# Three of a pair's weight sums added by DMA for one batch, and raw weights fetched from another queue

## The chip, the cores and the metric

The kernel runs on one core of one Trainium2 chip. The metric is the device time of one execution in microseconds (us). Times of several executions are given as a median; the profile is of one execution.

The engines are named as in the profile: PE is TensorE's matmul, PEld its loading of weights, DVE is VectorE, ACT is ScalarE, POOL is GpSimd, SP is SyncE, which here issues DMAs only. Each engine works through its own queue in order.

## The reference

Attention with a hash mask, then a Fourier mixing block with a two-layer network. Cut to what matters:

```python
# B, H, S, D = 4, 8, 768, 64; proj is 64 x 6; w_ch1 is 512 x 2048, w_ch2 is 2048 x 512
mask   = bucket(q @ proj)[:, :, :, None] == bucket(k @ proj)[:, :, None, :]   # 6 sign bits each
scores = where(mask, q @ k.T / 8, -1e9)
attn   = softmax(scores) @ v
x      = attn laid out as (B, S, 512)
mixed  = real(fft(fft(x, axis=1), axis=2))
u      = x + mixed
un     = (u - mean(u)) / sqrt(var(u) + 1e-6)
out    = u + relu(un @ w_ch1) @ w_ch2
```

The two network weights arrive as 64-bit floats and are narrowed on the chip; the other inputs are 32-bit floats.

## The kernel before

**Attention.** For each batch `b` (0 to 3), `attention(b)` goes through four pairs of heads (`n = 4 * b + t`), and in each pair through six chunks `c` of 128 keys. One chunk is one step of the generator. `weigh(n, c)` makes the scores of both heads for all 768 queries on TensorE (line 869), takes their exponential on ScalarE into a `pk` tile (line 873), and, for pairs that are not in `LITE = (0, 1, 2, 3, 4)`, multiplies by the hash mask on VectorE (line 879). In the `LITE` pairs the mask is put into the scores by a matmul with bits. There are two `pk` tiles (`NPK = 2`), used in turn, 128 partitions by 2 x 2 x 385 values, of which 384 of each 385 are weights.

The weights of a chunk go two ways. `values` multiplies them with v on TensorE (line 890). And their sum over all keys is needed for the softmax: VectorE adds the chunks into the tile `acc` (line 964; 128 x 1536 values, one buffer), for chunk 1 as the sum of the first two chunks' tiles, for later chunks as `acc` plus the new tile. In batch 0 the addition is made in two halves, and the last chunk is left to TensorE. When the six chunks are done, TensorE adds `acc` over the keys with `ones` (line 908), and `scale` divides by the sum and writes the tile `x` (lines 915 to 929).

**Mixing.** `mix(b)` runs beside `attention(b + 1)`: a fixed number of its steps is taken after each step of the attention. It folds `x`, makes the two Fourier transforms by matmuls (lines 1062 and 1091), normalises, and runs the network in `mlp7`, in which both products are made by the seven-product scheme of Strassen and Winograd: `inner` for the first layer (line 1366) and `outer7` for the second (line 1246). `spread` makes the reciprocal deviations `rs`, partly on GpSimd (lines 1127 and 1128). The seven operands that come from the first layer's weights are made on VectorE in `quarters` (lines 1164 to 1167), for batch 0 just ahead of their use, and are stored to the DRAM tile `ad` by SP; later batches fetch them back through a ring (`w<-ad`, line 1339). The second layer's operands go the same way through `bd` (lines 1217 and 1251).

**Raw weights.** The class `Arrival` fetches raw 64-bit weights, 512 KB at a time, into a few raw buffers (`zraw`, `fraw`) and narrows each with `narrow` (ScalarE lines 639, 646 and 647, VectorE lines 631 to 644). `convert(i)` narrows slice `i` and then issues the fetch of slice `i + depth` into the buffer that it has read, so that this DMA waits for the last instruction on that buffer. `weights1` does so for the first layer beside `attention(0)`, with seven raw buffers; its first seven fetches are issued by SP. `weights2` does so for the second layer beside batch 1's attention, with two raw buffers. All further fetches are issued by GpSimd (line 685). Besides these, GpSimd's queue carries in this part of the run the `rs` instructions, one small memset of `F` and the stores of batch 0's output (line 1000).

**Loads.** `load(n + 1)` is called at the start of pair `n` and issues q, k and v of the next pair from SP (lines 556, 562 and 570): in all 14 DMAs, most of them of 48 or 96 KB in short runs.

**Order.** In the part that holds `prepare(0)`, `attention(0)` and `weights1`, the order on PE, DVE, ACT and POOL is the order of the program, by a `manual_schedule`; SP is not in that list. From batch 1's attention on, a planner that simulates the engines orders each engine's queue, and the scores and values of later pairs are given a higher priority (`behind`). The order is fixed when the program is built.

Of the kernel before, what the change touches and what calls it, by code (L numbers as in the profile page):

```python
# [17 lines left out]
ALU = mybir.AluOpType  # L18
# [7 lines left out]
NT = S // P  # L26
# [453 lines left out]
def _main(  # L480
# [13 lines left out]
    nc = tc.nc  # L494
# [13 lines left out]
    def wt(shape, dtype, tag, name, bufs=2):  # L508
        return work.tile(shape, dtype, tag=tag, name=name, bufs=bufs)
# [110 lines left out]
    def narrow(dst, raw, col, low=None):  # L620


        lo, hi = (raw[..., i] for i in range(2))
        t = lo.bitcast(F32)
        if low is None:

            low, t = lo, hi.bitcast(F32)
        di = dst.bitcast(I32)


        nc.vector.tensor_scalar(
            di, hi, 3, (1 << 30) - 1,
            op0=ALU.logical_shift_left, op1=ALU.bitwise_and,
        )
        nc.vector.scalar_tensor_tensor(
            di, hi, -(1 << 30), di, op0=ALU.bitwise_and, op1=ALU.bitwise_or
        )

        nc.scalar.activation(low, lo.bitcast(U32), AF.Copy, scale=2.0**-29)
        if len(di.shape) == 2:  # L640
            nc.vector.tensor_tensor(di, di, low, op=ALU.add)
        else:
            for i in range(di.shape[1]):
                nc.vector.tensor_tensor(di[:, i], di[:, i], low[:, i], op=ALU.add)

        nc.scalar.activation(t, hi, AF.Abs)
        nc.scalar.activation(
            t, t, AF.Relu, bias=least, scale=-1.0, accum_out=strange[:, col : col + 1]
        )
# [22 lines left out]
    class Arrival:  # L672
# [19 lines left out]
        def convert(self, i, low=None):  # L692
            if self.wide:
                dst = self.slices[i][0]
                raw = self.raws[i % self.depth].bitcast(I32)
                if len(dst.shape) == 2:
                    raw = raw.rearrange("p (n w) -> p n w", w=2)
                else:
                    raw = raw.rearrange("p (s n w) -> p s n w", w=2, n=dst.shape[-1])
                narrow(dst, raw, self.col + i, low)  # L700
            self.fetch(i + self.depth, nc.gpsimd)

    def weights1():
        slices = [
# [139 lines left out]
    @contextmanager  # L844
    def behind():

        with tc.issue_after(last[0].ins), tc.high_priority(offset=AHEAD):
            yield
# [36 lines left out]
    def values(n, c, pk, oos):  # L885

        for g in range(2):
            w = HALF + 1 - g
            for h in range(2):
                nc.tensor.matmul(  # L890
                    oos[g][h * D : (h + 1) * D, 0:w], nat["v", n][:, (2 * c + h) * D : (2 * c + h + 1) * D],
                    pk[:, g, h, 0:w], start=(c == 0), stop=(c == NT - 1),
                )

    def scale(n, oos, sums):


        x = xs[n // NPAIR][:, n % NPAIR]
        vs = wt([P, 1], F32, "vs", f"vs{n}")
        nc.scalar.copy(vs, oos[0][:, HALF : HALF + 1])  # L900
        halves = [x[:, g * HALF : (g + 1) * HALF] for g in range(2)]
        for g, xg in enumerate(halves):
            nc.scalar.activation(xg, oos[g][:, 0:HALF], AF.Identity, bias=vs)

        ps = pt([P, HALF], f"sum{n}")
        for i, part in enumerate(sums):
            for j in range(4):
                nc.tensor.matmul(
                    ps[32 * j : 32 * j + 32, :], ones, part[:, j // 2, j % 2],
                    start=(i == 0), stop=(i == len(sums) - 1),  # L910
                )


        rt = wt([P, S], F32, "rt", f"rt{n}", 1)
        nc.vector.transpose(rt[:, 0:HALF], ps)
        rc = wt([P, HALF // 32], F32, "rc", f"rc{n}")
        nc.vector.tensor_scalar(rc, rt[:, 0:HALF:32], S * EPS, None, op0=ALU.add)
        nc.vector.reciprocal(rc, rc)
        yield
        rr = wt([P, 2, HALF // 32], F32, "rr", f"rr{n}")  # L920
        for g in range(2):
            for i in range(4):
                j = 2 * g + i // 2
                nc.scalar.copy(rr[32 * i : 32 * i + 32, g], rc[32 * j : 32 * j + 32])  # L924
        nc.vector.transpose(
            rt.rearrange("p (j i) -> p j i", i=32),
            rr.rearrange("p g j -> p (g j)")[:, :, None].broadcast_to([P, S // 32, 32]),
        )
        nc.vector.tensor_tensor(x, x, rt, op=ALU.mult)

    def attention(b):
        xs[b] = wt([P, NPAIR, S], F32, "x", f"x{b}")
        pending, scales = [], []

        def finish():
            n, c, pk, oos, sums = pending.pop(0)
            with behind() if n >= NPAIR and t is not None else nullcontext():
                values(n, c, pk, oos)
            if c == NT - 1:
                scales.append(scale(n, oos, sums))  # L940
                next(scales[-1])

        for t in range(NPAIR):
            n = NPAIR * b + t
            half = fold(b, 0) if t == NPAIR - 1 else iter(())
            if 1 < n + 1 < NPAIR * B:
                load(n + 1)
            ahead = prepare(n + 1) if n + 1 < NPAIR * B else iter(())
            oos = [ps_o.tile([P, 512], F32, tag="o", name=f"oo{n}_{g}") for g in range(2)]
            acc = wt([P, 2, 2, HALF], F32, "acc", f"acc{n}", 1)  # L950
            first = None
            for c in range(NT):
                pk = weigh(n, c)
                new = pk[:, :, :, 0:HALF]
                sums = [acc]
                if c == 0:
                    first = new
                elif c == NT - 1 and b == 0:

                    sums.append(new)  # L960
                else:

                    for g in (0, 1) if b == 0 else (slice(0, 2),):
                        nc.vector.tensor_tensor(  # L964
                            acc[:, g], (first if c == 1 else acc)[:, g], new[:, g],
                            op=ALU.add,
                        )

                for sc in scales:
                    next(sc, None)  # L970
                scales.clear()
                while pending:
                    finish()
                for sc in scales if b else ():
                    next(sc, None)
                pending.append((n, c, pk, oos, sums))
                if c > (3 if b == 1 else 2):
                    next(half, None)
                if c > 0:
                    next(ahead, None)  # L980
                yield
        t = None
        while pending:
            finish()
        for sc in scales:
            next(sc, None)
# [202 lines left out]
    def weights2():  # L1189

        slices = []
        for half in range(2):
            for r in range(HF // 2):
                for hi, first in ((0, B11), (1, B21)):
                    c = half * HF // 2 + r + hi * HF

                    step = 1 if hi else T1 - B11
                    dst = w2f[:, 0 : 7 * QB].rearrange("p (i r n) -> p i r n", i=7, n=HD)
                    slices.append(
                        (dst[:, first : first + step + 1 : step, r],  # L1200
                         moe_w_ch2[c * P : (c + 1) * P, :])
                    )
        arrival = Arrival(slices, [zt2[:, i] for i in range(2)], NDC * DFF // WC)
        for half in range(2):
            for i in range(arrival.depth) if half == 0 else ():
                arrival.fetch(i, nc.gpsimd)
            for i in range(HF):
                arrival.convert(half * HF + i)
                yield
                if i % 2:  # L1210
                    b11, b21, b22, t4, t1, t2, t3 = (q[:, i // 2] for q in right7)
                    nc.vector.tensor_tensor(t3, b22, t1, op=ALU.subtract)
                    nc.vector.tensor_tensor(t1, t1, b11, op=ALU.subtract)
                    nc.vector.tensor_tensor(t2, b22, t1, op=ALU.subtract)
                    nc.vector.tensor_tensor(t4, b21, t2, op=ALU.subtract)
            for i in range(7):
                nc.sync.dma_start(bd[half, i], right7[i])
            if half == 0:
                yield
# [350 lines left out]
```

## Time and profile before

| | |
|---|---|
| three executions | 1104.36, 1105.67, 1106.46 us |
| median | 1105.67 us |
| the profiled execution's own time | 1106.46 us |
| its span in the profile | 1104.7 us |
| mean granted TensorE clock | 0.991 of full speed |
| busy in the span: PE, DVE, ACT, POOL | 1050.9, 790.0, 500.3, 63.1 us |
| moved by DMA | 103.13 MB, mean 93 GB/s |

The span is what the profile covers; the execution's time holds 1.76 us more around it. Busy time of an engine counts its instructions, not its waits. In rows by stretches the columns are the stretch, its length, the busy time of PE, PEld, DVE, ACT and POOL with the number of instructions, the granted clock, the mean busy share of the 16 DMA engines, and GB/s. In rows of waits, the instruction that waited stands left of the arrow and what released it right, then the total in us, how often, and the longest. In rows of DMA issues the last column is the median time from issue to landing. In rows in order of time, the idle time before an instruction stands in brackets with what ended it. The stages follow from the lines: batch 0's attention to about 125 us, batch 1's from there to 416, batch 2's to 676, batch 3's to 933, and the rest is batch 3's mixing alone.

### The profile page before, as it was taken

The numbers are of one execution on the slowest core, as the hardware profiler recorded it, in microseconds if no ns is written. First come the engines' busy times: TensorE is split into PE (matmuls) and PEld (weight loads), VectorE is DVE, ScalarE is ACT, GpSimd is POOL, SyncE is SP. The second block draws the span as 40 slices with busy tenths as digits, with TensorE's granted clock in tenths as the row PEclk, the third lists the DMA queues.
The fourth block names the chain that finished last, engine by engine and source line by source line (L and its number), as shares of the span: only waits on it lengthen the run. The fifth ranks groups of instructions, "written<-read, shape, count | busy, mean of one in ns | idle before, by whom it ended". The sixth has DMA issues, their size and how long they took to land.

```text
span 1104.7 us, 14065 instructions
## 1 busy us (share of the span) xinstructions
PE 1050.9 (95%) x4893; PEld 636.6 (58%) x4893; DVE 790.0 (72%) x1326; ACT 500.3 (45%) x1055; POOL 63.1 (6%) x141
## 2 busy tenths in 40 slices
PE   6989888999989999999999999999999999999996
PEld 3334354445744675545664576645674569768575
DVE  5779968979598977786758785975856785644353
ACT  5869556654267324354426424354315532340420
POOL 0000000002000020010000011001000002100000
PEclk9989999999999999999999999999999999999998
DMA  8744534261046262313144134213032205122301
GB/s 225 201 99 96 101 106 109 99 196 26 20 130 183 73 192 52 63 58 76 26 152 110 49 67 167 44 38 91 20 109 85 69 26 172 53 82 91 119 20 42
DMA packets 175567, 103.13 MB, mean 93 GB/s; under 512 B 129408, under 2 KB 162816, under 8 KB 175488
## 3 DMA queue, kind: packets, MB, share of 16 engines
q1 hardware_dynamic: 168400, 83.93, 28.8%
q0 software_dynamic: 5520, 17.83, 5.2%
q8 instruction: 41, 0.67, 0.2%
q10 hardware_dynamic: 1568, 0.39, 0.2%
q14 instruction: 38, 0.31, 0.1%
HBM read 81.14 MB, written 20.97 MB: 92 GB/s over the span
## 4 chain that ended last, share of the span: by engine, by line
PE 56%; DVE 8%; ACT 3%; issue 1%; DMA 1%; DVEq 0%; ACTq 0%
PE o L1246 20%; PE h_p L1366 19%; PE oo L890 6%; PE sc L869 5%; PE cs L1062 2%; DVE pk L879 2%; PE A L1091 2%; PE B L1091 1%; DVE acc L964 1%; ACT rr L924 1%; DMA zraw<-in_moe_w_ch_dram 1%; PE un L1117 1%; DVE w L1258 1%; PE bits L804 1%; DVE h L1232 1%
## 5 line engine op out<-in xcount | busy, mean ns | idle before, releaser
L1246 PE MATMUL o<-w,h 128*128 128x256 f32 x1152 | 259.4, 382 | 1.1 <-ACT tq L1265 0.7
L1246 PEld LDWEIGHTS o<-w,h 128*128 128x128 f32 x1152 | 216.3, 190 | 43.5 <-issue 4.6
L873 ACT ACTIVATE pk<-sc 128x768 f32<-128x768 f32 x192 | 148.0, 808 | 82.4 <-PE sc L869 63.9
L1366 PE MATMUL h_p<-x,w 128*128 128x384 f32 x448 | 163.1, 494 | 3.6 <-ACT h L1388 2.3
L890 PE MATMUL oo<-pk,vn 128*64 128x385 f32 (+1 forms) x768 | 156.9, 503 | 3.6 <-DVE pk L879 3.0
L869 PE MATMUL sc<-qt,kt 64*128 64x384 f32 x768 | 155.3, 507 | 3.3 <-ACT pk L873 3.0
L879 DVE SCALAR_TENSOR_TENSOR pk<-qb,kb,pk 128x768 f32<-128x768 bf16 x132 | 128.9, 1012 | 29.1 <-ACT pk L873 28.9
L1366 PEld LDWEIGHTS h_p<-x,w 128*128 128x128 f32 x448 | 82.0, 190 | 71.0 <-ACT pk L873 5.4
L964 DVE TENSOR_TENSOR acc<-acc,pk 128x1536 f32<-128x1536 f32 (+1 forms) x72 | 105.7, 1482 | 6.6 <-ACT pk L873 6.1
L1366 PE MATMUL h_p<-w 128*128 128x384 f32 x288 | 105.5, 489 | 2.2 <-ACT w L1403 2.2
L890 PEld LDWEIGHTS oo<-pk,vn 128*64 128x64 f32 x768 | 49.7, 137 | 98.6 <-issue 71.8
L869 PEld LDWEIGHTS sc<-qt,kt 64*128 64x128 f32 x768 | 67.0, 188 | 48.7 <-issue 24.8
L1366 PEld LDWEIGHTS h_p<-w 128*128 128x128 f32 x288 | 53.7, 190 | 41.7 <-ACT w L1403 3.5
L1276 ACT COPY tq<-o 128x256 f32<-128x256 f32 x24 | 8.9, 373 | 105.2 <-PE o L1246 105.2
L1258 DVE SCALAR_TENSOR_TENSOR w<-o,rs,w 128x256 f32<-128x256 f32 x56 | 26.8, 479 | 41.6 <-PE o L1246 41.6
L1246 PE MATMUL o<-w 128*128 128x256 f32 x176 | 42.3, 383 | 1.4 <-DVE w L1258 1.3
L1392 DVE TENSOR_TENSOR h<-h 128x384 f32<-128x384 f32 x32 | 17.8, 555 | 31.9 <-ACT h L1391 31.8
L1265 ACT COPY tq<-o 128x256 f32<-128x256 f32 x24 | 8.9, 371 | 69.3 <-PE o L1246 69.2
L1000 POOL DMA_DIRECT2D out_dram<-w x30 | 16.3, 546 | 388.7 <-issue 293.2
L1246 PEld LDWEIGHTS o<-w 128*128 128x128 f32 x176 | 32.8, 190 | 8.8 <-DVE w L1258 2.9
L1399 DVE TENSOR_TENSOR h<-h 128x384 f32<-128x384 f32 x32 | 17.7, 553 | 26.8 <-ACT h L1398 26.8
L1292 DVE TENSOR_TENSOR tq<-tq,o 128x256 f32<-128x256 f32 x24 | 10.0, 418 | 34.7 <-PE o L1246 34.7
(170 smaller groups left out, 1350.7 us busy)
## 6 DMA issues: line engine op xcount, KB each, us to landing
w<-ad SPq DMA_DIRECT2D x168, 128.0 KB, 2.0
w<-bd SPq DMA_DIRECT2D x42, 512.0 KB, 4.4
zraw<-in_moe_w_ch_dram POOLq DMA_DIRECT2D x21, 512.0 KB, 4.1
bd<-w SPq DMA_DIRECT2D x14, 512.0 KB, 3.8
vn<-in_v_dram SPq DMA_DIRECT2D x32, 192.0 KB, 3.5
qn<-in_q_dram SPq DMA_DIRECT2D x120, 48.0 KB, 2.4
kn<-in_k_dram SPq DMA_DIRECT2D x60, 96.0 KB, 3.3
ad<-tq SPq DMA_DIRECT2D x8, 512.0 KB, 3.0
```

Source lines behind the costliest of these rows:

```text
L869: last[0] = nc.tensor.matmul(ps[:, h, 0:HALF], kt[rows, ks], qt[rows, qs], start=kb is not None, stop=True,)
L873: nc.scalar.activation(pk[:, g, :, 0:HALF], ps[:, :, 0:HALF], AF.Exp, scale=SCALE)
L879: nc.vector.scalar_tensor_tensor(w, qb[:, h].rearrange("p (g s) -> p g s", g=2), kb[:, h, c : c + 1], w, op0=ALU.is_equal, op1=ALU.mult,)
L890: nc.tensor.matmul(oos[g][h * D : (h + 1) * D, 0:w], nat["v", n][:, (2 * c + h) * D : (2 * c + h + 1) * D], pk[:, g, h, 0:w], start=(c == ...
L964: nc.vector.tensor_tensor(acc[:, g], (first if c == 1 else acc)[:, g], new[:, g], op=ALU.add,)
L1062: nc.tensor.matmul(ps[:, pc + 2 * lo : pc + 2 * hi - 1 : 2], z[:, cp, pc, par, t * P : (t + 1) * P], ch[:, cp, pc, lo:hi], start=(cp == 0) ...
L1091: nc.tensor.matmul(ps[:, cols], F[:, par, k, t, j * P : (j + 1) * P], sq[:, t, k, cols], start=(t == 0), stop=(t == 1),)
L1246: nc.tensor.matmul(ps, a[:, r], right7[i][:, r], start=start and r == 0, stop=r == HF // 2 - 1, skip_group_check=not start,)
L1258: nc.vector.scalar_tensor_tensor(t[:, cols], src, r, t[:, cols], op0=ALU.mult, op1=ALU.add)
L1366: nc.tensor.matmul(ps, left[:, k], right[i][:, k], start=start and k == 0, stop=k == 1, skip_group_check=not start,)
L1392: nc.vector.tensor_tensor(c21, c12, c21, op=ALU.add)
L1399: nc.vector.tensor_tensor(c22, c21, c22, op=ALU.add)
```

## The change

For batch 1 alone (pairs 4 to 7), the chunks 2, 3 and 4 of a pair are added into `acc` by a DMA that GpSimd issues and that adds what it reads to its destination. Chunk 1 and chunk 5 are added by VectorE as before, and the other batches are as before. All fetches of raw weights that GpSimd issued are issued by SP: the refills in `convert`, for both layers, and the first two fetches of the second layer.

```diff
@@ class Arrival, convert @@
                 narrow(dst, raw, self.col + i, low)
-            self.fetch(i + self.depth, nc.gpsimd)
+            self.fetch(i + self.depth, nc.sync)
@@ attention @@
                 if c == 0:
                     first = new
+                elif b == 1 and 1 < c < NT - 1:
+
+                    nc.gpsimd.dma_start(acc, new, accum_op=ALU.add)
                 elif c == NT - 1 and b == 0:
@@ weights2 @@
             for i in range(arrival.depth) if half == 0 else ():
-                arrival.fetch(i, nc.gpsimd)
+                arrival.fetch(i, nc.sync)
```

## The prediction

> **What bounds the kernel now.** I read the page first, then busy time by stretches of the run, then the waits of TensorE in the stretch that the change touches, then VectorE and TensorE in order of time there, then the DMA landings.
>
> The page's engine totals:
>
> ```profile
> PE 1050.9 (95%) x4893; PEld 636.6 (58%) x4893; DVE 790.0 (72%) x1326; ACT 500.3 (45%) x1055; POOL 63.1 (6%) x141
> ```
>
> TensorE sets the time: all that a change can win is its 53.8 us without work (1104.7 - 1050.9). Where that lies is in the busy time by stretches; after the length come PE, PEld, DVE, ACT and POOL:
>
> ```profile
> 125.00:416.00 291.00, 271.47 (x1258) 159.05 (x1252) 238.95 (x438) 146.77 (x314) 23.55 (x44) 0.99 0.41 114
> 416.00:676.00 260.00, 256.13 (x1190) 154.61 (x1188) 191.22 (x292) 109.76 (x235) 13.76 (x31) 1.00 0.32 84
> 676.00:933.00 257.00, 253.78 (x1175) 155.43 (x1172) 186.17 (x288) 102.39 (x218) 13.57 (x30) 1.00 0.24 70
> ...
> 140.00:157.00 17.00, 14.21 (x91) 7.82 (x92) 11.88 (x20) 9.96 (x20) 0.00 (x0) 1.00 0.29 86
> 180.00:233.00 53.00, 46.66 (x173) 22.73 (x172) 45.45 (x85) 31.71 (x69) 3.17 (x6) 0.97 0.42 147
> 300.00:352.00 52.00, 47.33 (x189) 24.61 (x187) 49.43 (x95) 36.49 (x79) 2.64 (x5) 1.00 0.50 132
> 352.00:395.00 43.00, 41.96 (x197) 25.40 (x196) 39.86 (x74) 16.08 (x36) 2.17 (x4) 1.00 0.40 131
> ```
>
> Batch 1's attention, with batch 0's mixing beside it, is 125 to 416 us. TensorE idles 19.5 us there, against 3.9 and 3.2 in the two stages after it, which do the same work without the weight conversions. VectorE is 82% busy, and 49.4 of 52 us between 300 and 352. This is the one stage where VectorE is near to binding, and the stage that the change edits.
>
> **What is removed.** For batch 1, chunks 2, 3 and 4 of each of four pairs lose their VectorE addition: 12 instructions. The row of the adding line in this stage, and one place where TensorE stands behind such an addition:
>
> ```profile
> L964 DVE TENSOR_TENSOR acc<-acc,pk x16: 1714/1750/1759, 143.9 to 383.0; 128x1536 f32<-128x1536 f32 x16
> 147.05 1.75 DVE L964 TENSOR_TENSOR acc<-acc,pk 128x1536 f32<-128x1536 f32 x1
> 148.72 0.55 DVE L808 TENSOR_SCALAR bt<-bits 128x384 bf16<-128x384 f32 x1
> 149.33 1.16 PE L1062 MATMUL cs<-ch,z 128*128 128x127 f32 x8 [1.26 <-DVE bt L808]
> ```
>
> An addition holds VectorE for 1.67 us, from its start to the next instruction's (147.05 to 148.72). Twelve give 20.0 us, and VectorE falls from 239 to 219 us of 291. Only what ends an idle time of TensorE counts. Three do so visibly: the 1.26 us above; 1.28 us at 312.0, where TensorE waits for line 1165 at the end of a VectorE queue that is solid since 300.4 and holds the addition of 303.1; and 0.74 us at 391.9, at the end of a VectorE chain that holds the addition of 370.5. That is 3.3 us, the lower end. The upper end is TensorE's idle time after the first removed addition in each packed stretch: 2.8 us in 140 to 157, 0.5 at 222.7, 4.7 in 300 to 352, 1.0 in 352 to 395, in all 9.0. The rest (178 to 183, 231.9) comes from ScalarE standing behind a weight transfer, and stays. I take 5.0, nearer the end whose waits are named. What is late next is ScalarE's queue, which orders conversions, exponentials and copies.
>
> **What is added on the path of the weights.** Twelve accumulating DMAs from the pk tile to acc, 768 KB each (128 x 1536 x 4 bytes), issued by GpSimd. The trace has no such DMA. Nearest rows in this stage, and the whole run's row for the one load of this size:
>
> ```profile
> zraw<-in_moe_w_ch_dram POOLq DMA_DIRECT2D x16, 512.0 KB, 3.9
> bd<-w SPq DMA_DIRECT2D x14, 512.0 KB, 3.8
> ad<-tq SPq DMA_DIRECT2D x7, 512.0 KB, 3.0
> ...
> sq<-k_sq SPq DMA_DIRECT2D x1, 770.0 KB, 15.1
> ```
>
> Low end 3.8 us; high end 15.1, which was taken in the crowded first 40 us. Half as large again as 512 KB makes 5.8, and the destination is read too, so I take 7. The additions of a pair are a chain: chunk 3's DMA waits for chunk 2's landing, chunk 4's for chunk 3's, and VectorE's addition of chunk 5 for the last. And pk has two buffers, so the exponential of chunk c + 2 waits until chunk c's DMA has landed. The room before, from the start of the addition to that exponential: in the second pair 203.3 to 205.7 for chunk 2 is 2.4 us; in the first 143.9 to 151.5 is 7.5; in the third 267.2 to 298.9 is 31.7, in the fourth 348.9 to 365.2 is 16. At 7 us the second pair's exponential comes 4.6 us late, but its mask runs at 217.4 only, so that it hides. The first pair, which has no mask instructions and the shortest steps, has its chain land at 150.9, 157.9 and 164.9; the addition of chunk 5 (161.1) comes 3.8 us late, covered because its sum on TensorE starts at 184.9 only. I put down 0.5 us of loss for the whole chain; below nothing is excluded, since a longer hold cannot free anything. The loss at 15.1 us is in the first rival.
>
> The Trainium skill, "DMA: Bandwidth & Descriptors", section on the anatomy of one DMA, fits a GpSimd-issued DMA with 2.0 us plus bytes over 436 GB/s: an estimate of 3.8 us here, and this term would be 0. The same page's rules for kernel authors say that an accumulate reads its destination and writes it later, and must wait for the earlier DMA's semaphore: the serial chain above.
>
> **What is moved.** 16 weight fetches of this stage and nine of the first go from GpSimd's queue to SP's. GpSimd spent 0.53 us on each, now free. GpSimd must be clear of them, since it now stands waiting for masks and for landings: behind those waits lie only the rs instructions (254.7 to 269.7) and the output stores from 377 on. The chain at 267 could hold the last rs by one landing, 7 us; it is used at 290, so nothing. On SP a fetch stands behind the head loads (qn, kn, vn), the ad and bd stores and the ring fetches w<-ad, all of which wait in order for VectorE or TensorE. ScalarE waited 20.5 us for these transfers in 13 places:
>
> ```profile
> ACT zraw L639 <- DMA zraw<-in_moe_w_ch_dram: 20.5, 13, 4.1
> ```
>
> Of the 16, those of 168.5, 170.6, 327.2 and 332.0 meet SP while it issues or holds head loads (168.4 to 175.5, 323.8 to 330.9) or a store until 339.3. Bounds for each: 0, if it keeps its place and landing, and the 7.3 us that SP stood at 332.0 to 339.3. Earlier SP fetches landed in 6.1 and 9.9 us against 4.1 and 5.0 from GpSimd, but in the first 25 us. About a quarter of ScalarE's wait shows as idle TensorE (5.9 us: the idles at 178.7, 182.5, 231.9 and 351.0, against 23.2 with VectorE's share of 2.7). Four fetches later by 1 to 2 us make 6 us of wait, 1.5 us of TensorE; all four by 7.3 us make 7. They cannot gain more than those 5.9 us. In the first stage a fetch is seven conversions ahead of its use, and ScalarE and VectorE waited there 2.9 and 0.8 us: nothing.
>
> The skill's same page, section on issuing engines, holds that all queues run on the same 16 DMA engines and that the issuer only saves issue time; by it this term is 0. No run here shows the same fetch from both queues in the same stretch.
>
> **The sum.** -5.0 + 0.5 + 1.5 = -3.0 us. The profiled run took 1106.46 us (span 1104.7 and 1.76 around it), so 1103.5; it lay 0.8 above the median of 1105.67, so the forecast is 1102.7. About 0.2% (2.2 us) is what a measurement can tell from no change.
>
> **Rivals.** First, slower: the accumulating DMA is slow, and two pk buffers throttle the attention. It decides from about 8 us a DMA. At 10 us the first pair's landings are 153.9, 163.9 and 173.9, the last 7.0 us after the second pair's first exponential (166.9), which needs that buffer; I let half of this, 3.5 us, reach TensorE, whose order is fixed when the program is built and which then stands in front of what needs it. At 15.1 us they are 159.0, 174.1 and 189.2, 22.3 us after it: half is 11, and the second pair's chunk 2 lands at 218.4, past its mask at 217.4, for about 3 more with the exponential between. So 1102.7 + 3.5 to 1102.7 + 14, or 1106.2 to 1116.7, with 1111 in the middle. For it: only two buffers and the chain. Against: the 512 KB rows at 3 to 4 us. Chance 0.24.
>
> Second, slower: SP holds the fetches back. Its four late fetches cost up to 7 us instead of 1.5: 1102.7 + 5.5 = 1108.2. For it: SP stood 60.4 us in one wait for line 1167. Against: that wait ended at 313.3, between fetches. Chance 0.13.
>
> Third, no change: the removed additions were covered, only the named 3.3 us come back, and 0.5 and 1.5 go off: -1.3, or 1104.4. For it: TensorE is 93% busy even here. Chance 0.20.
>
> Forecast 0.43, with its own range 1096.7 (9.0 won, none lost) to 1103.4 (2.2 below the median). Over the cases the range is 1098 to 1112: it leaves out the slower half of the first rival and a gain beyond 7.7 us. Faster 0.43, same 0.20, slower 0.37.
>
> **What would show it.** VectorE's adding row in the stage down to 4 + 4 instructions; TensorE idle in the stage near 16.5 us; the accumulating row landing under 8 us; idle at 149, 312 and 392 gone; ScalarE's wait for zraw at 20 to 27 us. I am wrong if ScalarE's exponential waits for acc for more than about 5 us in all, or if landings exceed 10 us.

## The result and the profile after

The changed kernel takes 1111.49 us (median of four executions, 1109.01 to 1113.27), the kernel before 1105.84 us in the same comparison: a ratio of 1.0051, 95% interval 1.0028 to 1.0075. It is slower by about 5.7 us, where 3.0 us of gain were forecast. The profiled execution took 1113.27 us, its span is 1111.4 us and its mean granted clock 0.990. Behind line 960, the DMA addition, the changed kernel's line numbers are 3 higher than those of the kernel before: its VectorE addition is line 967.

The page's engine totals of the changed kernel:

```profile
PE 1052.8 (95%) x4893; PEld 640.7 (58%) x4893; DVE 771.8 (69%) x1314; ACT 499.5 (45%) x1055; POOL 64.0 (6%) x128
```

VectorE has lost its 12 additions and 18 us of work; TensorE makes as many matmuls as before. Of the 6.7 us by which the span is longer, 4.8 us are more idle time of TensorE (58.6 us and 53.8), and 1.9 us are slower matmuls. The busy time by stretches shows where (columns as before):

```profile
125.00:416.00 291.00, 265.43 (x1188) 156.50 (x1189) 215.22 (x415) 143.25 (x303) 28.68 (x37) 0.97 0.57 136
416.00:676.00 260.00, 256.14 (x1189) 155.09 (x1188) 190.56 (x290) 108.43 (x230) 13.57 (x29) 1.00 0.32 84
676.00:933.00 257.00, 253.80 (x1171) 154.47 (x1170) 186.58 (x288) 102.88 (x217) 13.57 (x29) 1.00 0.24 70
140.00:157.00 17.00, 17.00 (x113) 10.26 (x110) 2.95 (x7) 9.22 (x20) 3.09 (x3) 1.00 1.01 225
157.00:180.00 23.00, 18.39 (x85) 12.43 (x83) 18.66 (x35) 12.16 (x22) 0.00 (x0) 0.85 0.64 148
180.00:233.00 53.00, 45.23 (x154) 21.84 (x154) 37.00 (x73) 29.48 (x63) 3.81 (x3) 0.90 0.71 191
300.00:352.00 52.00, 47.31 (x197) 24.00 (x196) 45.59 (x91) 35.44 (x76) 1.28 (x1) 1.00 0.58 144
352.00:395.00 43.00, 38.77 (x179) 22.06 (x177) 33.34 (x65) 17.44 (x35) 5.00 (x5) 1.00 0.71 172
```

Batches 2 and 3 are as before. In the edited stage VectorE has indeed become looser, from 238.95 to 215.22 us of 291, and TensorE does less in the same time: 25.6 us idle instead of 19.5. Equal stretches do not hold quite the same work, since this profile enters the stage 4.2 us earlier (the last sum of batch 0 begins at 120.23 us, not 124.42). From that sum to the last one of batch 1 it takes 274.2 us, to 394.47, where the kernel before took 262.2, to 386.62.

The first stretch, 140 to 157, is the change at its best: the 1.26 us of idle time at 149.3 is gone and TensorE never rests. The next one gives it back: 4.6 us idle in 157 to 180 and a granted clock of 0.85, where the kernel before had 1.4 us and 1.00. In 180 to 233 it is 7.8 us and 0.90 instead of 6.3 and 0.97, and in 352 to 395 4.2 us instead of 1.0, at a full clock.

The rows of the VectorE addition in this stage, and the DMA issues there (KB each, median us from issue to landing):

```profile
L967 DVE TENSOR_TENSOR acc<-pk,pk x4: 1716/1746/1754, 134.5 to 338.8; 128x1536 f32<-128x1536 f32 x4
L967 DVE TENSOR_TENSOR acc<-acc,pk x4: 1715/1733/1759, 162.7 to 390.9; 128x1536 f32<-128x1536 f32 x4
```

```profile
acc<-pk POOLq DMA_DIRECT2D x12, 768.0 KB, 7.8
zraw<-in_moe_w_ch_dram SPq DMA_DIRECT2D x16, 512.0 KB, 4.0
bd<-w SPq DMA_DIRECT2D x14, 512.0 KB, 7.2
```

4 + 4 additions are left. An accumulating DMA lands after 7.8 us in the median (6.7 to 13.4), and the stores `bd<-w` beside it take 7.2 us instead of 3.8. ScalarE's wait for raw weights:

```profile
ACT zraw L639 <- DMA zraw<-in_moe_w_ch_dram: 14.5, 11, 4.1
```

It fell from 20.5 us, where 20 to 27 was expected. And the place where the first pair loses its time, VectorE and TensorE in order of time:

```profile
162.70 1.76 DVE L967 TENSOR_TENSOR acc<-acc,pk 128x1536 f32<-128x1536 f32 x1 [4.24 <-DMA acc<-pk]
164.97 1.01 DVE L1108 TENSOR_TENSOR x<-x,A 128x384 f32<-128x384 f32 x2
166.13 1.62 PE L1094 MATMUL A<-sq,F 128*128 128x193 f32 x4 [4.48 <-DVE x L1108]
```

Chunk 5's addition waits 4.24 us for the last of the pair's three landings. The next instructions in VectorE's queue, the mixing's line 1108 among them, need nothing of `acc`, but they stand behind it; TensorE needs line 1108 and is idle for 4.48 us. Then its matmuls take 1.62 us for four instead of 0.92: the clock is 0.50 between 166 and 172.

### The profile page after: what moved, and what is told of

Its sections match the earlier page's. It is cut to its first block, busy times and chain, and to the rows that moved or that the text cites. A ratio compares the mean times of both kernels' runs of the same rounds, so it can differ in the third digit from the quotient of the medians.

```text
span 1111.4 us, 14073 instructions
## 1 busy us (share of the span) xinstructions
PE 1052.8 (95%) x4893; PEld 640.7 (58%) x4893; DVE 771.8 (69%) x1314; ACT 499.5 (45%) x1055; POOL 64.0 (6%) x128
## 4 chain that ended last, share of the span: by engine, by line
PE 63%; DVE 12%; DMA 6%; ACT 5%; issue 2%; SPq 0%; DVEq 0%; ACTq 0%; POOLq 0%
PE o L1249 23%; PE h_p L1369 20%; PE oo L890 7%; PE sc L869 6%; DMA acc<-pk 3%; DVE pk L879 2%; DMA zraw<-in_moe_w_ch_dram 2%; PE A L1094 2%; PE cs L1065 2%; PE B L1094 2%; DVE acc L967 1%; ACT rr L924 1%; ACT pk L873 1%; DMA bd<-w 1%; PE bits L804 1%
## 5 line engine op out<-in xcount | busy, mean ns | idle before, releaser
L890 PE MATMUL oo<-pk,vn 128*64 128x385 f32 (+1 forms) x768 | 153.6, 499 | 3.0 <-DVE pk L879 2.6
L967 DVE TENSOR_TENSOR acc<-acc,pk 128x1536 f32<-128x1536 f32 (+1 forms) x60 | 84.7, 1427 | 4.7 <-DMA acc<-pk 4.2
L1295 DVE TENSOR_TENSOR tq<-tq,o 128x256 f32<-128x256 f32 x24 | 10.1, 420 | 34.9 <-PE o L1249 34.7
```

The lines of the kernel that those rows point to most:

```text
L890: nc.tensor.matmul(oos[g][h * D : (h + 1) * D, 0:w], nat["v", n][:, (2 * c + h) * D : (2 * c + h + 1) * D], pk[:, g, h, 0:w], start=(c == ...
L967: nc.vector.tensor_tensor(acc[:, g], (first if c == 1 else acc)[:, g], new[:, g], op=ALU.add,)
```

## The experiments

Two theories at first. **A:** the accumulating DMAs cost the time, by those who wait for them or by their traffic, and the fetches on SP gain. **B:** SP's queue costs the time. Later ones are stated with their runs. All times below are medians; "ratio" is to the kernel before on the same chip, with its 95% interval. That kernel's own median was 1105.0 to 1105.9 us in these comparisons, so a difference between two of them can be off by as much.

### One half of the change at a time

With SP's fetches and VectorE's additions:

```diff
-                elif b == 1 and 1 < c < NT - 1:
-
-                    nc.gpsimd.dma_start(acc, new, accum_op=ALU.add)
```

> The additions are all VectorE's again; the fetches stay on SP. Theory A (the cost is in the accumulating DMAs, and the first stage's lead of 4.2 us at its last sum, 120.2 against 124.4 us, comes from the fetches on SP): 1105.8 - 4.2, about 1102, with the last sum of batch 0 near 120. Theory B (the cost is SP's queue, which holds fetches and loads back in batch 1's stage, and the lead is chance): 1108 to 1111. If the two cancel, 1105 to 1106.

1097.98 us (1097.59 to 1098.37), ratio 0.9933 (0.9915 to 0.9952). That is below all that either theory expected. The fetches alone gain 7.9 us, and the DMA additions cost 13.5 (1111.49 - 1097.98).

With the DMA additions and GpSimd's fetches:

```diff
-            self.fetch(i + self.depth, nc.sync)
+            self.fetch(i + self.depth, nc.gpsimd)
...
-                arrival.fetch(i, nc.sync)
+                arrival.fetch(i, nc.gpsimd)
```

> The additions by DMA as in the changed kernel; the fetches on GpSimd again. Theory A: the first stage loses its lead of 4.2 us, and the fetches now stand behind the waits of the accumulating DMAs on GpSimd, so 1115 to 1118. Theory B: SP is freed and the time falls to 1104 to 1107.

1120.57 us (1119.34 to 1121.39), ratio 1.0135 (1.011 to 1.016), slower than theory A expected and far from B. Its waits:

```profile
ACT zraw L639 <- DMA zraw<-in_moe_w_ch_dram: 38.9, 15, 8.5
POOL zraw L685 <- DMA acc<-pk: 6.5, 1, 6.5
```

Here a fetch stands in GpSimd's queue behind an addition that waits for the landing before it, and ScalarE waits 38.9 us for raw weights. Theory B has fallen: moving the fetches away from GpSimd is the good half of the change, and beside DMA additions it is worth still more (9.1 us).

### Where the additions cost

The DMA additions in pairs 5 to 7 only:

```diff
-                elif b == 1 and 1 < c < NT - 1:
+                elif b == 1 and t > 0 and 1 < c < NT - 1:
```

> As the changed kernel, but the first pair of batch 1 is added by VectorE. Theory A1 (most of the loss is the first pair's chain of three landings, behind which VectorE stood 4.2 us and TensorE 4.5 us, with a granted clock of 0.85 in the next 23 us): 1111.5 - 4.5 - 1.7, about 1105. Theory A2 (most of the loss is in the transfers that the accumulating DMAs slow, at 217 to 221 and 371 to 375): 1109 to 1111.

1108.06 us (1105.81 to 1110.2), ratio 1.002 (1.0007 to 1.0034): 3.4 of the 13.5 us come back, between the two theories. No wait of VectorE for an addition's landing is left in this kernel's profile, and 10.1 us of cost remain, so that wait cannot be all.

All DMA additions, but chunk 5 of batch 1 summed on TensorE as in batch 0, so that nothing on VectorE waits for a landing:

```diff
-                elif c == NT - 1 and b == 0:
+                elif c == NT - 1 and b < 2:
```

> As the changed kernel, but batch 1's last chunk of each pair is left to TensorE, as in batch 0, so that no VectorE instruction waits for a landing. It adds 8 short matmuls a pair, 0.8 us by the row of line 908, 3.3 us for four pairs. Theory A1 (VectorE's queue blocked by its wait): the 4.2 us wait of VectorE is gone, and 1111.5 - 6.2 + 3.3, about 1108.6, with no VectorE idle over 1 us released by the accumulating DMA. Theory A2: the loss stays and the matmuls add to it, 1113 to 1115.

1099.27 us (1097.58 to 1100.38), ratio 0.9946 (0.9926 to 0.9965): 12.2 of 13.5 us come back, more than the waits of VectorE explain and more than either theory expected. The planner orders the queues anew in this run (the exponentials of ScalarE wait at most 1.6 us for a landing), so it does not tell the wait from the order. The same edit without any DMA addition:

> No DMA additions, all fetches on SP, and batch 1's chunk 5 summed on TensorE beside the sum of the others, as in batch 0. It is the run with DMA additions and chunk 5 on TensorE (1099.27 us) without its DMA additions. Theory A (what the DMA additions cost is that VectorE and others wait for them and their traffic; they bring nothing): 1094.5 to 1098.5 us, below 1099.27. If instead the 12 additions taken off VectorE are worth something once nothing on VectorE waits for a landing: over 1099.5 us.

1098.29 us (1097.33 to 1098.72), ratio 0.9937 (0.9921 to 0.9953): as fast as with chunk 5 on VectorE (1097.98). So moving that chunk is worth nothing by itself, and with it the DMA additions cost 1.0 us.

The traffic without the additions:

```diff
+    spare = tc.dram_tile([P, 2, 2, HALF], F32, name="spare")
...
+                if b == 1 and 1 < c < NT - 1:
+                    nc.gpsimd.dma_start(spare, new)
```

> All fetches on SP, VectorE adds all chunks as in the kernel before, and GpSimd issues 12 plain copies of 768 KB at the places of the DMA additions, from the same pk tiles to a spare tensor in DRAM that nobody reads: the traffic and the hold on pk without a wait of VectorE for a landing. Theory A1 (the cost is the order behind VectorE's waiting addition): 1098 to 1101 us. Theory A2 (the cost is the traffic, which delays the fetches, stores and loads that ScalarE waits for): 1103 to 1110 us, with zraw, kn or bd landings well over 5 us.

1098.3 us (1096.98 to 1098.76), ratio 0.9935 (0.9918 to 0.9951). Twelve plain copies of as many bytes cost nothing that can be measured. They are not the same load, though: they land in 4.0 us in the median and not 7.8, and their queue takes 10.4% of the DMA engines between 125 and 416 us, against 21.1% with the additions and 1.5% without either.

### Which of the moved fetches gain

SP for the first layer's fetches alone, and for the second layer's alone:

```diff
-        def __init__(self, slices, raws, col):
+        def __init__(self, slices, raws, col, queue=nc.sync):
...
-            self.fetch(i + self.depth, nc.sync)
+            self.fetch(i + self.depth, self.queue)
```

> No DMA additions; SP fetches the first layer's weights, GpSimd the second layer's. With both on SP the time was 1097.98 us, with both on GpSimd 1105.88: 7.9 us to divide. Theory F1, the gain lies in the first stage (the profile of the kernel before has its last sum of batch 0 at 124.42 us, with all fetches on SP at 119.87): 1098 to 1102 us. Theory F2, the gain lies beside batch 1, where SP's fetches of the second layer shorten ScalarE's wait for zraw from 20.5 to 11.2 us, and the first stage's lead is one execution's chance (the kernel with DMA additions and all fetches on GpSimd has that sum at 119.71 us too): 1103 to 1106 us.

1104.99 us (1103.19 to 1106.88), ratio 0.9998 (0.9987 to 1.0009): nothing.

> No DMA additions; GpSimd fetches the first layer's weights, SP the second layer's. F1: 1102 to 1106 us, with the wide spread of the kernel before (1102.31 to 1108.99). F2: 1098 to 1101 us. If both stages share the gain, both this run and the other split lie near 1102.

1098.9 us (1098.05 to 1103.15), ratio 0.9943 (0.9927 to 0.9959). The gain lies beside batch 1 (F2). The lead of 4.2 us that the changed kernel's profile has at the end of batch 0's attention is no gain in time. The last sum of batch 0 begins at 124.42 us in the profile of the kernel before and at 124.55 in this run's (1103.15 us, the highest of its six), but at 119.71 in the profile of the kernel with DMA additions and GpSimd's fetches: with GpSimd's fetches ScalarE waited 2.9 us for a landing in two of these three executions and 0.8 in the third. The profile of the run with SP for the first layer alone has the lead (120.02), but by the sum of the second pair 1.1 us of it are left (248.81 and 249.92), and it takes 1105.31 us.

### The order of the queues

The planner fixes each engine's order when the program is built, and it plans differently when VectorE has less to do. Set beside the kernel of the first experiment (1097.98 us), the changed program has 73 of 2618 instructions of TensorE, 115 of 993 of ScalarE and 179 of 1315 of VectorE in other places. The next runs hold this order fixed, by edges that order two instructions of one engine and wait for nothing; `at` is read from a table of positions. TensorE, ScalarE and VectorE are held; SP's order stays the planner's and moves with theirs (36 of its 526 DMAs stand elsewhere in the first such run than in the changed kernel), so that "order" below takes in SP's too:

```diff
+        for one, two in zip(at, at[1:]):
+            tc.add_manual_dep(ins[two], ins[one].name, info, reason="pin")
```

**Theory W:** the additions cost by the work that waits for them. **Theory O:** the planner's other order costs. For the runs without additions the further edit is

```diff
-                    nc.gpsimd.dma_start(acc, new, accum_op=ALU.add)
+                    pass
...
-        nc.vector.tensor_scalar(rc, rt[:, 0:HALF:32], S * EPS, None, op0=ALU.add)
+        nc.vector.tensor_scalar(rc, rt[:, 0:HALF:32], 1.0 if n // NPAIR == 1 else S * EPS, None, op0=ALU.add)
```

> The changed kernel with all its DMA additions, but TensorE, ScalarE and VectorE take their instructions in the order that the kernel with SP's fetches alone has (1097.98 us); edges of order alone are added, no waits. In the changed kernel the planner, with 12 additions fewer on VectorE, put 73 of 2618 TensorE, 115 of 993 ScalarE and 179 of 1315 VectorE instructions in other places. Theory W (the cost is that work waits for landings of the accumulating DMAs): the waits stay, 1108 to 1113 us. Theory O (the cost is the planner's other order, which brings the narrowing of raw weights ahead on ScalarE's queue, where it waits for fetches): 1097 to 1102 us.

1103.49 us (1102.45 to 1104.32), ratio 0.9975 (0.9962 to 0.9988): between the two theories.

> Batch 1's chunks 2 to 4 are added by nobody (their 12 additions are left out of the sums, and 1.0 stands in place of the small constant that is added to batch 1's sums), and TensorE, ScalarE and VectorE take their instructions in exactly the order of the changed kernel. Theory W: with no DMA additions nothing waits for them, 1094 to 1099 us. Theory O: the order costs as before, 1105 to 1112 us. A time half way would divide the 13.5 us between the two.

1098.61 us (1094.99 to 1100.68), ratio 0.9934 (0.9913 to 0.9956): theory W's range, though near its upper end.

> The same additions left out, in the order of the kernel with SP's fetches alone. It shows what the removal of 12 VectorE additions can bring at most with nothing in its place: the prediction's first term said 5.0 us. Both theories: 1092 to 1097.5 us, if VectorE's relief reaches TensorE; 1097.5 to 1099 if it doesn't.

1092.56 us (1091.96 to 1095.77), ratio 0.9892 (0.9871 to 0.9914).

Neither theory was right alone. All fetches on SP, median us:

| chunks 2 to 4 of batch 1 | order planned for VectorE's additions | order of the changed kernel |
|---|---|---|
| added by VectorE | 1097.98 | not run |
| added by nobody | 1092.56 | 1098.61 |
| added by DMA | 1103.49 | 1111.49 |

Down the first column: taking the additions off VectorE (and their hold on the `pk` tiles) gains 5.4 us, and giving them to DMAs costs 10.9. Across: the changed kernel's order costs 6.0 us with no DMA addition at all, and 8.0 with them. Each difference is of two medians whose executions spread by 1 to 6 us.

How the order and the traffic meet is seen in the second pair, on SP, ScalarE and TensorE in order of time. The changed kernel:

```profile
211.63 0.33 SPq L685 DMA_DIRECT2D zraw<-in_moe_w_ch_dram  x1
219.67 0.67 ACT L639 ACTIVATE zraw<-zraw 128x512 int32<-128x512 uint32 x1 [4.08 <-DMA zraw<-in_moe_w_ch_dram]
220.75 1.65 PE L1369 MATMUL h_p<-zraw,w 128*128 128x384 f32 x2 [3.10 <-ACT w L1406]
```

The same order without the additions, on SP and ScalarE:

```profile
207.32 0.33 SPq L685 DMA_DIRECT2D zraw<-in_moe_w_ch_dram  x1
211.70 0.68 ACT L639 ACTIVATE zraw<-zraw 128x512 int32<-128x512 uint32 x1 [0.44 <-DMA zraw<-in_moe_w_ch_dram]
```

With 12 additions fewer on VectorE the planner put the narrowing of a slice close behind its fetch on ScalarE. A fetch that is there after 4.4 us holds ScalarE for 0.44 us; beside a DMA addition (issued at 208.43, landed at 219.36) the same fetch takes 8.0 us and holds ScalarE for 4.08, and behind it stands the copy, line 1406, that TensorE waits for; its clock is then 0.50 until about 230. The fourth pair has another such case: a load of `kn` goes out at 362.38, lands after 10.1 us, and ScalarE begins on it at 372.52, after 3.19 us of idle time; without the additions it goes out at 351.03, lands after 4.6 us, and ScalarE begins on it at 359.09 with none.

Where the order costs without any DMA addition is seen by the sums of the pairs (line 908). Against the other order the last sum of batch 0 begins 1.1 us later, which no addition can have caused, and the pairs then lose 0.8, 1.8, 0.0 and 4.4 us. In the second pair TensorE stands 2.13 us (at 217.73) behind a narrowing that has waited 1.35 us for its fetch. In the fourth it stands 2.81 us (at 325.24) behind ScalarE, where a narrowing could begin only when its fetch had landed (319.36 and 319.27), and the clock is 0.71 for the next 5.8 us; in the other order TensorE stands there 1.52 us and in the second pair's place not at all.

SP's fetches in the order of the kernel before (from which the order planned for SP's fetches differs in 33 instructions of TensorE, 64 of ScalarE and 101 of VectorE):

> No DMA additions, all fetches on SP, and TensorE, ScalarE and VectorE take their instructions in the order of the kernel before, so that SP's queue is the only difference. It divides the 7.9 us that SP's fetches gain. If the queue itself gains (ScalarE waits less for zraw because SP's fetches land sooner): 1098 to 1101 us. If the planner's other order gains: 1103 to 1106 us.

1100.45 us (1097.42 to 1101.92), ratio 0.9945 (0.9924 to 0.9965). The queue itself (with the planner's order on SP) gains 5.5 us, and the order that the planner makes of it for the other engines 2.5 more; the 2.5 are less sure, since two of these six executions took 1097.42 and 1097.6 us. In order of time, one buffer's turn in the kernel before:

```profile
298.13 0.77 ACT L647 ACTIVATE zraw<-zraw,least 128x512 f32<-128x512 f32 x1
299.28 0.62 POOL L685 DMA_DIRECT2D zraw<-in_moe_w_ch_dram  x1 [29.57 <-ACT zraw L647]
303.20 0.69 ACT L639 ACTIVATE zraw<-zraw 128x512 int32<-128x512 uint32 x1 [1.60 <-DMA zraw<-in_moe_w_ch_dram]
```

and in this run:

```profile
292.66 0.77 ACT L647 ACTIVATE zraw<-zraw,least 128x512 f32<-128x512 f32 x1
293.55 0.35 SPq L685 DMA_DIRECT2D zraw<-in_moe_w_ch_dram  x1
297.10 0.68 ACT L639 ACTIVATE zraw<-zraw 128x512 int32<-128x512 uint32 x1 [0.96 <-DMA zraw<-in_moe_w_ch_dram]
```

From the end of line 647 to the next narrowing it takes 4.30 us by GpSimd and 3.67 by SP, and the fetch after it 4.30 and 3.74. All 14 refills are like it: from line 647's end to the landing each is shorter by 0.1 to 1.7 us, 0.6 in the median. With two raw buffers such a delay can become a wait of ScalarE, whose total went from 20.5 to 14.0 us.

### What the additions' own 10.9 us are

The run with DMA additions in the other order shows two places where TensorE stands for them. One is the first pair's, as above (VectorE waits 4.1 us, TensorE 4.48 behind it). The other is in the second pair, on GpSimd, ScalarE and TensorE in order of time:

```profile
200.23 1.27 POOL L960 DMA_DIRECT2D acc<-pk  x1 [43.05 <-DVE pk L879]
208.59 0.81 ACT L873 ACTIVATE pk<-sc 128x768 f32<-128x768 f32 x1 [5.40 <-DMA acc<-pk]
209.30 0.47 ACT L1406 COPY w<-h_p 128x384 f32<-128x384 f32 x1
209.82 2.93 PE L1369 MATMUL h_p<-zraw,w 128*128 128x384 f32 x4 [4.57 <-ACT w L1406]
```

An addition of chunk 2 goes out at 200.23 and is landed at about 208.5. The exponential of chunk 4 writes the same `pk` tile and waits 5.40 us for it; the copy of line 1406 stands behind the exponential, and TensorE behind the copy. Against the run without additions in the same order, the sum of a pair (line 908) is 6.1 us later in the first pair (183.04 and 176.91), 10.8 in the second (250.16 and 239.35) and 10.8 in the third and fourth. But 1.5 us of it are there at the last sum of batch 0, ahead of any DMA addition (120.48 and 118.95). So 4.6 us arise in the first pair and 4.7 in the second, which hold the two places, and nothing after them. Three runs divide it, in the same order, with the DMA additions in some pairs only:

```diff
-                elif b == 1 and 1 < c < NT - 1:
+                elif n in (5, 6, 7) and 1 < c < NT - 1:
```

> Fetches on SP, the order of the kernel with SP's fetches alone on TensorE, ScalarE and VectorE; the additions of chunks 2 to 4 by DMA in pairs 5, 6 and 7, by VectorE at their old places in pair 4. If the cost lies at the two places that the trace shows (pair 4: +5.7 of waits, less some 3 us of VectorE's relief; pair 5: +4.7): the wait in pair 4 goes and the one in pair 5 stays, 1100 to 1103 us. If the traffic costs everywhere: over 1102 us, with waits in pairs 6 and 7.

1101.04 us (1100.27 to 1102.5), ratio 0.9958 (0.9946 to 0.9971).

> As the run before, with the DMA additions in pair 4 alone. Waits at the two places: VectorE's wait of about 4 us and TensorE's wait behind it stay, less the relief of pair 4, 1099.5 to 1102 us. Traffic everywhere: a quarter of the 10.9 us less a quarter of the relief, under 1099.5 us.

1100.93 us (1099.67 to 1102.72), ratio 0.9957 (0.9939 to 0.9975).

> As the runs before, with the DMA additions in pairs 6 and 7 alone, where the trace shows no wait of TensorE for them. Waits at the two places: nothing waits, and the relief of these two pairs (about 2 of 5.4 us) is a gain, 1095 to 1097.5 us, below every kernel so far with all its additions. Traffic everywhere: 1098 to 1101 us.

1095.35 us (1094.5 to 1095.79), ratio 0.9908 (0.9886 to 0.9929). From 1097.98 us: pair 4 adds 2.9 us after its own relief, pairs 5 to 7 add 3.1, and pairs 6 and 7 alone take off 2.6. In the waits of that last kernel only GpSimd itself stands for an addition's landing, and no instruction of VectorE, ScalarE or TensorE does:

```profile
POOL acc L960 <- DMA acc<-pk: 4.5, 1, 4.5
```

This is the fastest of all kernels here that do all their additions, 10.3 us (0.9%) under the kernel before. A third `pk` tile, which might take away the second place, was not tried.

## Why the prediction was wrong, by its steps

From the kernel before to the changed one the runs give, in us and taken in this order: SP's queue -5.5, the planner's order with SP's fetches -2.5, VectorE's relief -5.4, the DMA additions +10.9, the planner's order with VectorE relieved +8.0; together +5.5 of the 5.7 measured. The forecast had -5.0 + 0.5 + 1.5.

**VectorE's relief, -5.0: right.** It measures -5.4 when nothing takes the additions' place and the order is kept (the runs' profiles differ by 0.9 us already at the last sum of batch 0).

**The chain of DMAs, +0.5: wrong, +10.9.** The 7 us taken for a landing were near the 6.9 us (median) of the run that isolates them and the 7.8 us of the changed kernel; what failed is the cover, twice. "The addition of chunk 5 comes 3.8 us late, covered because its sum on TensorE starts at 184.9 only": the lateness is right (4.2 us), but it looked at who reads the sum, and not at what is queued behind the waiting addition on VectorE. "At 7 us the second pair's exponential comes 4.6 us late, but its mask runs at 217.4 only, so that it hides": right again in size (5.4 us), and again the queue was left out, this time the copy of line 1406 behind the exponential on ScalarE. The first rival had the mechanism of two `pk` tiles, but its place, the second pair's first exponential, does not wait for a landing in the changed kernel (166.53). The hold came in the second pair, at a landing of 8.3 us (200.23 to 208.51), where the rival had set it only at 15.1. That its middle, 1111, met the time is luck: it is made without the 8.0 us of the order and the 7.9 of the fetches, which nearly cancel. It let half of a lateness reach TensorE; of the waits of 4.1 and 5.4 us, 4.6 and 4.7 us reached the pair's sum. What neither the forecast nor the rival had is the clock: behind the two waits it was 0.50 from 166 to 172 us and from 209.8 to 213.0, by my estimate from these figures some 3 and 1.6 us more.

**The order, no term: +8.0.** The prediction said that the order is fixed when the program is built, and took it for the same order. It is fixed from what the planner sees, and 12 instructions fewer on VectorE were enough to move the narrowing nearer to its fetches. "What is late next is ScalarE's queue" was the right engine without a price. 6.0 us of it come without any DMA addition; the other 2.0 come where that order meets their traffic.

**The fetches on SP, +1.5: wrong in sign, -7.9.** "In the first stage ... nothing" holds. Beside batch 1 the prediction looked for fetches held in SP's queue and set the gain of the issue at nothing; but a fetch with two buffers is a closed loop (the next fetch waits for the narrowing, and the narrowing for the fetch), and the 0.6 us a turn stand in all 14 refills. The bound "they cannot gain more than those 5.9 us" holds for the queue alone (5.5) and not with the order that follows from it. The second rival, SP holding the fetches back, does not occur beside batch 1 when no DMA addition is there. The Trainium skill, "DMA: Bandwidth & Descriptors", rules for kernel authors, says that spreading DMAs over issuers only saves the sequencer's issue time; the runs agree in that the median landing of a 512 KB fetch is nearly the same from either queue (3.9 and 3.8 us), but the time saved per turn, 0.6 us, is more than the 0.2 to 0.3 us between the two issue durations (0.53 to 0.62 and 0.33 to 0.35), and it decided the stage.

**What would show it.** The additions' row (4 + 4) and the idle times at 149 and 392 went as said; that at 312 fell only from 1.28 to 0.62 us (at 315.53). TensorE's idle time in the stage is 25.6 us and not 16.5; ScalarE's wait for raw weights is below its range; landings exceed 10 us (13.4), which was named as a sign of being wrong. ScalarE's waits for a DMA addition are only 3.7 us in all, under the 5 us named: the sign was set on the wrong engine for the first pair.

## What to carry to other kernels

When work moves from an engine to a DMA, price the wait by what is queued behind the instruction that will wait for the landing, on its engine, and not by when its result is read; then put such a DMA only where the trace shows that this queue has slack, as in pairs 6 and 7 here. Where a planner orders the queues, an edit of the load of one engine reorders the others: compare the two orders, and pin one of them to tell the edit's own price from the order's. Plain fetches that refill few buffers belong on the queue with the shortest turn, and above all not behind instructions that wait for landings.

## What the runs showed of the hardware

An accumulating DMA of 768 KB between two tiles landed after 6.7 to 13.4 us, and took about twice the DMA engines' time of a plain copy of the same bytes to DRAM (21.1 and 10.4% of the stage, less 1.5% of other work on that queue); with the order of the queues held, a 512 KB fetch beside it took 8.0 us instead of 4.4, and the median `bd<-w` store of the stage 7.2 instead of 4.4.

After an idle time of 4.48 us TensorE's granted clock was 0.50 from 166 to 172 us, and 0.99 from 172 on. The Trainium skill, "TensorE: Matmul & The Clock Gate", Part 1, has this as a gate that goes to half rate after a window of about 3.4 us without work and back after as long with work; the windows run freely, and the runs agree: after 4.54 us of idle time in the run with pair 4 alone the first four matmuls still took 0.98 us, and the next four 1.62. The return took nearly 6 us in the changed kernel, and the length of the idle time alone did not decide: after 3.10 us (at 220.75) the clock was 0.50 until about 230, after 3.14 us (at 374.62) it stayed 1.00. The first of these is shorter than the page's window; the ends of matmuls, from which idle times are counted, are modelled, and no run here settles it.
